# An S4 state-space layer's forward and backward pass: the first quarter of one long transform placed in front of K's return from DRAM, and some transfers issued by another engine

## The chip, the cores and the metric

The kernel runs on one core of a Trainium2 chip. A core has a matrix engine (TensorE, in the profile PE, with its weight loads shown apart as PEld), a vector engine (VectorE, DVE), a scalar engine (ScalarE, ACT), GpSimd (POOL) and SyncE (SP, which here only issues transfers). Transfers between DRAM and the on-chip memory run on 16 DMA engines; SyncE, ScalarE and GpSimd each have a queue in which they issue them, in program order and between their other instructions. Every engine works through its own list of instructions in order and waits on semaphores for the others.

The metric is the time of one execution in microseconds on the device. Three runs of the kernel before took 821.86, 829.3 and 836.6 us; the median is 829.3. The profile comes from one further execution of 824.42 us.

## The reference

One function computes a block and its gradients. `u` is [1, 2048, 512], the state size is N = 128, the feed-forward width F = 1792, and the inputs are bfloat16.

```python
xn = layernorm(A_u)
K  = einsum("dn,dnl,dn->dl", C, exp(dt*A*l), dt*B).real      # a filter of 2048 taps per channel
y  = irfft(rfft(pad(xn)) * rfft(pad(K)))[:L] + xn * Dskip     # long convolution along the sequence
g  = silu( silu(xn @ w1) @ w2 )
out = A_u + y * g
# returned: out, and the gradients of A_u, A_re, A_im, B_re, B_im, C_re, C_im, log_dt, Dskip, w1, w2
```

The backward pass needs two more long convolutions (the gradients to K and to xn), sums over all 2048 positions for the parameters of the state space, and four matrix products for the feed-forward part.

## The kernel before, in words

The kernel computes the Fourier transforms as matrix products with tables of sines and cosines. Positions are split as 128 partitions by T = 16 tiles; frequencies in four quarters `kt` of 512 each; a spectrum quarter is a tile of [128, 2 (real, imaginary), 4, 512] in bfloat16, 1 MB. The order of the work is written out by hand: generators (`gen_xt`, `gen_kt`, `gen_d` and so on) each emit the next piece at a `next`, and the loops of the stages decide whose turn it is. What stands first in that order stands first on every engine's list.

- Stage 1: layer norm, feed-forward forward, the sine tables `TFd` and `TId` in DRAM, and the base powers of the state space, `XYd` in DRAM. It leaves `DS`, the product of the incoming gradient and the gate, on the chip.
- Stage 2 (lines 924 to 1005): for four blocks `b` of channels, `open_tables` (L727) loads base powers into `X`; `chunk_tables` (L769 to 774, and L782 to 789 for the two tables `CY` and `Y`) multiplies them out on VectorE; `chunk_K` (L808) forms the filter K on TensorE; `gen_xt` and `gen_yt` (L878 to 897) transpose the tables and store them as `XTd` and `YTd`. Beside it `fwd_classes` (L919) transforms xn, one quarter at a time; `radix` (L931) finishes a quarter on VectorE with `rad4` (L88) and stores it as `UXd` (L935). `store_K` writes K to DRAM and `load_K` (L833) reads it back in another order as `K_b`, half of the 22 loads on SyncE's queue and half on GpSimd's. Then VectorE adds `Dskip` to one row of `K_b` (L1003). `gen_masks` (L178) is some 60 small VectorE operations.
- Stage 3 (L1143, `gen_kt`): for each quarter, TensorE transforms `K_b` (`fwd_eo`, L1046; ScalarE copies the results out, L1048); VectorE adds even and odd halves (`add_eo`, L1056 to 1061), multiplies by the spectrum of xn (`cplx_mul`, L106 to 110) and runs a radix step (L91 to 98) into `BY`.
- Stage 4 (L1254): eight steps of the inverse transform (`inv_mm`, L1070) give the convolution's result, from which VectorE makes `DO`, the output and more (L1215 to 1217). Woven in is `gen_d` (L1225), the same transform, product and radix step for `DS`, four quarters, into `BK`; the spectra of K and DS are stored as `KXd` and `DXd`.
- Stage 5 (L1441): products for w2's gradient (`Dw2`, L1431) from `DO`; inverse transform of `BK` (L1467), summed over positions by `gs` (L1462) into `dKgd` in DRAM, from where `Gt` is loaded on GpSimd's queue (L1496); `Prod` (L1387) loads `KXd` and `DXd` and forms the third convolution's spectrum `BG` on VectorE. Then the slabs (`Slabs`, L1548) sum for the state-space parameters, with the inverse transform of `BG` and the rest of `Dw2` beside them.
- Stage 6 (L1760): the backward pass of the feed-forward part (`Bwd`), and `gen_ssm_final` (L1303), which loads the sums `Snd` (L1347) and finishes the parameters' gradients on VectorE.

On-chip memory is a stack of pools on a left and a right side (`lo`, `ro`); a tile that is given the place of an older one waits until that one's last reader or transfer is done. A pool with `bufs=1` gives tiles of one `tag` the same place in turn.

Of the kernel before, what the change touches and what calls it, by code (L numbers as in the profile page):

```python
# [11 lines left out]
BF16 = mybir.dt.bfloat16  # L12
# [101 lines left out]
class Stack:  # L114


    def __init__(self, k, side):
        self.k, self.side, self.open_ = k, side, []
# [18 lines left out]
def kernel(ctx, tc, A_u, A_A_re, A_A_im, A_B_re, A_B_im, A_C_re, A_C_im, A_log_dt, A_Dskip, B_x, B_w1, B_w2, grad_out,  # L137
# [26 lines left out]
    k.UXd = XS("UXd"); k.DXd = XS("DXd"); k.KXd = XS("KXd")  # L164
    k.Snd = dr.tile([2, 2, D, N], F32, name="Snd")
# [758 lines left out]
def stage_2(k):  # L924
# [23 lines left out]
    for b in range(NB):  # L948
        Kg = chunk_K(k, b, k.tabs[b])
        Tc, Tn = k.gc.get(b + 1), k.gt.get(b + 1)  # L950
        gx = gen_xt(k, k.xs, b)
        gy = [gen_yt(k, k.xs, i) for i in range(4 * b, 4 * b + 4)]
        sl = [y for g in gy for y in (gx, gx, gx, g)][1:]
        if b == 2:
            sl, gy2 = [None if g in gy else g for g in sl], gy
        if b == 3:
            for _ in Kg:
                pass
            break
        if b:  # L960
            open_tables(k, b + 1, nc.sync)
        fr = front(b + 1) if b else iter(())
        for j, g in enumerate(sl):
            if j % 3 == 1:
                next(fr, None)
            if j < 4:
                next(Tc, None)
            if j == 0 and b < 2:
                next(k.gt[b])
            if j == 4 and b < 2:  # L970
                ld_tab(k, b + 2)
            if j % 2 == 0:
                next(Kg, None)
            if g:
                next(g)
            if b == 0 and j in (1, 3):
                radix(j // 2)
            if j in (4, 6, 8, 10, 12, 14):
                next(Tn)
        for _ in fr:  # L980
            pass
    store_K(k)
    next(k.gt[2])
    for g in gy2:
        next(g)
# [17 lines left out]
    nc.vector.tensor_tensor(out=K_b[0:1, 0, :], in0=K_b[0:1, 0, :], in1=Dsk[:], op=ALU.add)  # L1003
    ro.close("uw", "cyb")
    return K_b, sl
# [101 lines left out]

def gen_kt(k, kq, K_b, UX):

# [5 lines left out]
    def front(kt):  # L1115
        TFs = k.TFs
        TN = neg_tf(k, kq, TFs, False)
        k.TFs = ld_tf(k, (kt + 1) % 4, nc.scalar)
        st[kt] = kq.tile([P, 2, 2, 2, W], BF16, name="Ak", tag="A")
        yield from fwd_eo(k, st[kt], K_b, TFs, TN, False)  # L1120
# [22 lines left out]
def stage_3(k, K_b, sl):  # L1143
# [3 lines left out]
    k.by = lo.open("by")  # L1147
    k.BY = k.by.tile([P, 4, 2, 4, W], BF16, name="BY", tag="B")
    kq = k.kq = lo.open("kq")
    UX = ld_ux(k, kq, 0)  # L1150
    for n, _ in enumerate(gen_kt(k, kq, K_b, UX)):
# [72 lines left out]

def gen_d(k, bk, dp):  # L1225
# [3 lines left out]
    k.BK = []  # L1229
    for kt in range(4):  # L1230
# [15 lines left out]
        B_ = (bk if kt else k.tf2).tile([P, 2, 4, W], BF16, name="BK", tag=f"BK{kt}" if kt else "TFs")  # L1246
# [7 lines left out]
def stage_4(k):  # L1254
# [9 lines left out]
    for t0 in range(0, T, TS):  # L1264
        if t0 % 4 == 0:
            for _ in range(2):
                next(gd)
# [15 lines left out]
        if t0 % 4 == 0:  # L1283
            next(gd)
            if t0 + 4 < T:
                next(gd)
        elif t0 + 2 < T:
            for _ in range(3):
                next(gd)
        else:  # L1290
            next(gd); next(gd)
# [4 lines left out]
        if t0 + 4 == T:  # L1296
            k.w2 = Dw2(k)
            for ft in range(3):
                k.w2.load(ft, nc.gpsimd)
    ro.close("y2")  # L1300


def gen_ssm_final(k, fp):  # L1303
# [83 lines left out]
class Prod:  # L1387


    def __init__(self, k, pw):  # L1390
        self.k, self.ld, self.pl = k, {}, [(k.kq, "A", k.kq, "X"), (k.kq, "UXl", pw, "dXl")]
# [49 lines left out]
def stage_5(k):  # L1441
# [5 lines left out]
    pr = Prod(k, pw)  # L1447
    pr.load(0, k.KXd)
# [16 lines left out]
    for t0 in range(0, T, TS):  # L1465
# [8 lines left out]
        if t0 == 0:  # L1474
            pr.load(1, k.KXd)
        kt = t0 // 4
        if t0 % 4 == 0:
            pr.mul(kt)
        else:
            pr.rad(kt, BG[:, kt])  # L1480
            if kt < 2:
                pr.load(kt + 2, k.KXd)
# [370 lines left out]
```

## Time and profile before

| | us |
|---|---|
| runs shown (3) | 821.86 to 836.6, median 829.3 |
| profiled execution | 824.42 |
| its span, first to last instruction | 822.6 |
| TensorE busy | 676.0 (82%) |
| VectorE busy | 622.5 (76%) |
| ScalarE busy | 435.4 (53%) |
| GpSimd busy | 87.9 (11%) |
| mean granted TensorE clock | 0.929 |

| stretch (us from the start) | what runs |
|---|---|
| 175 to 285 | stage 2: tables, K, transform of xn |
| 285 to 308 | K to DRAM and back |
| 308 to 390 | stage 3: transform of K, `BY` |
| 390 to 480 | stage 4: first inverse transform, `DO`, transform of DS, `BK` |
| 457 to 640 | stage 5 |
| 640 to 822 | stage 6 |

Times below are microseconds from the first instruction of the profiled execution. In a line of the timeline the first number is the start and the second the length; the brackets at its end hold how long the engine had stood idle and what released it. A line may stand for several instructions of one form (x16). "SPq", "ACTq" and "POOLq" are the issues of transfers on the three queues; a transfer's own duration is shown only as "landing", from issue to the end, and only for GpSimd's queue.

### The profile page before, as it was taken

What the parts mean: (1) busy time and instruction counts of PE and PEld (TensorE: products, weight loads), DVE (VectorE), ACT (ScalarE), POOL (GpSimd) and SP (SyncE); (2) the same over time, 40 slices, a digit from 0 to 9 for tenths busy, and PEclk for the clock granted to TensorE, in tenths of its full rate; (3) what the DMA queues carried; (4) which work ended last, traced back from release to release, by engine and by line L of the source; (5) the groups of instructions that cost most, each with busy time, mean ns of one, the idle gap of its engine ahead of it and who ended that gap; (6) DMA issues with size and microseconds to landing.
All of it is one profiled execution on the core that took longest, in us unless ns stands there. A gap on an engine that the chain in (4) does not pass through costs nothing.

```text
span 822.6 us, 13686 instructions
## 1 busy us (share of the span) xinstructions
PE 676.0 (82%) x5284; PEld 345.2 (42%) x5284; DVE 622.5 (76%) x1015; ACT 435.4 (53%) x530; POOL 87.9 (11%) x113
## 2 busy tenths in 40 slices
PE   5868968987478539886999899679887999798998
PEld 2424534434356425342444343234333445344454
DVE  6899999549996992999899999645575458688710
ACT  4888889955569455342444221135444755466221
POOL 1251431020000030000000001102022200001010
PEclk9989979899879878889999999799998999899999
DMA  9557867796788489784788987879999695557561
GB/s 283 203 173 243 293 218 243 269 319 215 255 247 270 116 221 360 288 331 154 239 303 312 366 346 294 186 188 220 269 261 247 157 259 160 156 158 224 179 203 62
DMA packets 154359, 195.19 MB, mean 237 GB/s; under 512 B 37539, under 2 KB 114566, under 8 KB 147862
## 3 DMA queue, kind: packets, MB, share of 16 engines
q1 hardware_dynamic: 144870, 166.26, 65.3%
q0 software_dynamic: 5488, 14.61, 5.8%
q10 hardware_dynamic: 3936, 13.44, 4.8%
q8 instruction: 41, 0.67, 0.3%
q14 instruction: 24, 0.20, 0.1%
HBM read 110.10 MB, written 80.50 MB: 232 GB/s over the span
## 4 chain that ended last, share of the span: by engine, by line
PE 22%; DVE 17%; DMA 12%; ACT 4%; issue 3%; SPq 1%; POOL 0%; DVEq 0%; ACTq 0%; POOLq 0%
PE ps_w L1806 6%; PE ps_v L1070 4%; PE ps_dx L1729 3%; PE ps_da L1690 3%; DMA XTl<-XTd 3%; PE ps_w L1431 2%; DMA Gt<-dKgd 2%; DVE cm_t L106 2%; DMA TIs<-TId 1%; DMA UXl<-UXd 1%; PE ps_V L1584 1%; DMA AW<-akd 1%; PE pt_dh L1712 1%; DMA YTl<-YTd 1%; DVE cm_t L108 1%
## 5 line engine op out<-in xcount | busy, mean ns | idle before, releaser
L579 PE MATMUL ps_h<-XNT,W 128*128 128x512 bf16 x224 | 59.5, 414 | 13.4 <-ACT hs L582 13.4
L1070 PEld LDWEIGHTS <-TIs 128*128 128x128 bf16 x384 | 38.7, 102 | 66.2 <-issue 24.6
L1046 PEld LDWEIGHTS <-TFs 128*128 128x128 bf16 x336 | 34.3, 103 | 62.9 <-issue 28.6
L1431 PE MATMUL ps_w<-DO_all,AW 128*128 128x512 bf16 x224 | 57.1, 405 | 2.9 <-DVE DO_all L1215 2.9
L555 PE MATMUL ps_o<-W,aT 128*128 128x512 bf16 x224 | 54.8, 394 | 2.5 <-DVE ak L76 2.5
L1046 PE MATMUL ps_f<-K_b,TFs 128*128 128x512 bf16 x160 | 43.8, 433 | 14.5 <-DVE K_b L1003 8.1
L1690 PE MATMUL ps_da<-DOT,W2T 128*128 128x512 bf16 x224 | 53.6, 382 | 1.5 <-ACT DOT L1670 1.1
L1729 PE MATMUL ps_dx<-W1T,dhT 128*128 128x512 bf16 x224 | 54.6, 387 | 0.2 <-DMA W1T<-in_B_w_dram 0.2
L1691 DVE TENSOR_TENSOR dhT<-ps_da,sd 128x1024 bf16<-128x1024 f32 x28 | 34.1, 1222 | 23.1 <-ACT sd L133 17.3
L880 ACT COPY XT<-pt_xt 128x1024 bf16<-128x1024 bf16 (+1 forms) x44 | 40.9, 1005 | 17.1 <-DMA XTd<-XT 8.4
L1595 DVE TENSOR_TENSOR T<-Vb,YTl 128x2048 bf16<-128x2048 bf16 x16 | 19.6, 1224 | 39.0 <-ACT Vb L1586 38.9
L1806 PE MATMUL ps_w<-dhc,xn 128*128 128x448 bf16 x256 | 49.1, 352 | 0.0
L1586 ACT CAST Vb<-ps_V 128x1024 bf16<-128x1024 f32 x32 | 31.7, 1013 | 30.8 <-PE ps_V L1584 19.8
L1046 PE MATMUL ps_f<-DS,TFs 128*128 128x512 bf16 x176 | 40.6, 379 | 3.6 <-ACT dEO L1048 2.2
L1070 PE MATMUL ps_v<-BG,TIs 128*128 128x512 bf16 x128 | 33.2, 420 | 8.2 <-DVE BG L97 6.8
L579 PEld LDWEIGHTS <-W 128*128 128x128 bf16 x224 | 22.4, 104 | 38.7 <-issue 21.4
L1738 ACT ACTIVATE dxn<-dxn,c,rstd 128x512 f32<-128x512 f32 x16 | 13.0, 814 | 45.6 <-DVE c L1737 45.6
L1048 ACT CAST Ak<-ps_f 128x1024 bf16<-128x1024 f32 x16 | 16.0, 1014 | 39.1 <-PE ps_f L1046 23.0
L555 PEld LDWEIGHTS <-aT 128*128 128x128 bf16 x224 | 22.8, 102 | 32.1 <-issue 8.3
L1714 ACT COPY dhk<-pt_dh 128x1024 bf16<-128x1024 bf16 x28 | 28.0, 1001 | 14.3 <-PE pt_dh L1712 14.3
L1431 PEld LDWEIGHTS <-AW 128*128 128x128 bf16 x224 | 21.3, 103 | 33.4 <-issue 14.0
L919 PE MATMUL ps_f<-xn,TFs 128*128 128x512 bf16 x128 | 31.8, 401 | 4.2 <-ACT XU L920 2.6
(296 smaller groups left out, 1511.5 us busy)
## 6 DMA issues: line engine op xcount, KB each, us to landing
TIs<-TId SPq DMA_DIRECT2D x24, 512.0 KB
XTd<-XT SPq DMA_DIRECT2D x20, 512.0 KB
XTl<-XTd SPq DMA_DIRECT2D x16, 640.0 KB
UXl<-UXd SPq DMA_DIRECT2D x8, 1024.0 KB
hTd<-hs SPq DMA_DIRECT2D x28, 256.0 KB
akd<-ak SPq DMA_DIRECT2D x28, 256.0 KB
TFs<-TFd ACTq DMA_DIRECT2D x7, 1024.0 KB
hsb<-hTd SPq DMA_DIRECT2D x28, 256.0 KB
```

The lines of the kernel that those rows point to most:

```text
L555: nc.tensor.matmul(out=pso[:], lhsT=aT[:, ft, tt * P:(tt + 1) * P], rhs=W2[:, ft, :], start=(ft == 0), stop=(ft == FT - 1))
L579: nc.tensor.matmul(out=ps[:, j], lhsT=W1[:, dk, ft * P:(ft + 1) * P], rhs=XNT[:, dk], start=(dk == 0), stop=(dk == DK - 1))
L880: nc.scalar.copy(out=XT[:, j0:j0 + len(ks)], in_=pt[:, 0:len(ks)])
L919: nc.tensor.matmul(out=ps[:, c, :], lhsT=TFs[:, t1 + 4 * j, c, :], rhs=src[:, t1 + 4 * j, :], start=(j == 0), stop=(j == 3))
L1046: nc.tensor.matmul(out=ps[:, c, :], lhsT=tab(j), rhs=src[:, t1 + 4 * j, :], start=(n == 0), stop=(n == 4 * len(terms) - 1))
L1070: nc.tensor.matmul(out=ps[:, j, :], lhsT=TIs[:, j, 2 * kt + c, :], rhs=B[kt][:, c, (t0 + j) % 4, :], start=(kt == 0 and c == 0), stop=(kt ...
L1431: nc.tensor.matmul(out=ps[:], lhsT=A[:, t, :], rhs=k.DO[:, t, :], start=(t == 0), stop=(t == T - 1))
L1586: nc.scalar.copy(out=self.V[i][:, g2], in_=ps[:].rearrange("p b c n -> p c b n"))
L1690: nc.tensor.matmul(out=ps[:, j], lhsT=self.W2T[:, dk, ft * P:(ft + 1) * P], rhs=self.DOT[tc_][:, dk], start=(dk == 0), stop=(dk == DK - 1))
L1691: nc.vector.tensor_tensor(out=self.dhT[:, f0:f0 + 2, :], in0=ps[:], in1=sd[:], op=ALU.mult)
L1729: nc.tensor.matmul(out=psx[:], lhsT=dhT[:, ft, t % 4 * P:(t % 4 + 1) * P], rhs=self.W1T[:, ft, :], start=(ft == 0), stop=(ft == FT - 1))
L1806: nc.tensor.matmul(out=ps[:], lhsT=k.xn[:, t, dk * P:(dk + 1) * P], rhs=ch[i][:, t, :], start=(t == 0), stop=(t == T - 1))
```

## The change

Five things are moved; the number of instructions on TensorE and VectorE stays the same.

1. The first quarter of DS (transform, product, radix) leaves stage 4 and stands in stage 2 behind `load_K` and ahead of the `Dskip` addition and the masks (`gen_d0`, new). It uses the table quarter 0 that the first quarter of K also uses, so one load of `TFs` and one of `UXl` go. Its result goes to DRAM (`BKd`, new) and comes back in stage 4. Its two stores are issued by GpSimd.
2. In stage 2, table `Y` of block 2 and its `gen_yt` stand in block 2's own loop; before, they came after K. The radix steps of the third and fourth quarter of xn come right after `store_K`, ahead of table `Y` of block 3; the masks come after the `Dskip` addition.
3. The stores of xn's spectrum (`UXd`) and the loads of `X` for blocks 2 and 3 are issued by GpSimd; before, by SyncE.
4. Stage 4 has three quarters of DS in place of four, the loads for `Dw2` and for the first product of `Prod` stand at step 10, and that product is computed at step 14; in stage 5 the rest of `Prod` moves up accordingly.
5. In `gen_ssm_final` the loads of `Snd` stand four steps earlier.

```diff
     def radix(b):
...
-        nc.sync.dma_start(k.UXd[b], XU[:])
+        nc.gpsimd.dma_start(k.UXd[b], XU[:])
...
         sl = [y for g in gy for y in (gx, gx, gx, g)][1:]
-        if b == 2:
-            sl, gy2 = [None if g in gy else g for g in sl], gy
...
-            open_tables(k, b + 1, nc.sync)
+            open_tables(k, b + 1, nc.gpsimd)
...
-            if j == 0 and b < 2:
+            if j == 0:
                 next(k.gt[b])
...
     store_K(k)
-    next(k.gt[2])
-    for g in gy2:
-        next(g)
+    radix(2); radix(3)
     next(k.gt[3])
-    lo.close("xc", "ko", "sa")
-    k.do = lo.open("do")
+    for _ in range(3):
+        next(gx)
+    ro.close("uw", "cyb"); lo.close("xc", "ko", "sa")
+    k.do = lo.open("do"); k.by = lo.open("by"); kq = k.kq = lo.open("kq")
     K_b = k.do.tile([P, T, D], BF16, name="K_b", tag="DO")
-    Dsk = uw.tile([1, D], BF16, name="Dsk_b", bufs=1)
+    UX = ld_ux(k, kq, 0)
+    Dsk = kq.tile([1, D], BF16, name="Dsk_b")
     nc.sync.dma_start(Dsk[:], k.ins["Dskip"].unsqueeze(0))
     load_K(k, K_b)
-    sl = iter(sl)
-    for n in range(8):
-        next(next(sl))
-        if n == 1:
-            radix(2)
-        if n == 3:
-            radix(3)
-            k.masks = gen_masks(k, uw)
-            next(k.masks)
-    next(k.masks)
+    TN = neg_tf(k, kq, k.TFs, False)
+    d0 = gen_d0(k, kq, UX, TN)
+    for _ in range(4):
+        next(d0)
+        next(gx)
+    next(d0)
     nc.vector.tensor_tensor(out=K_b[0:1, 0, :], in0=K_b[0:1, 0, :], in1=Dsk[:], op=ALU.add)
-    ro.close("uw", "cyb")
-    return K_b, sl
+    for _ in gen_masks(k, kq):
+        pass
+    return K_b, UX, TN, iter([gx] * 4 + gy)
...
+def gen_d0(k, dp, UX, TN):
+    nc = k.nc
+    A = dp.tile([P, 2, 2, 2, W], BF16, name="dEO", tag="A")
+    yield from fwd_eo(k, A, k.DS, k.TFs, TN, False)
+    XD = dp.tile([P, 2, 4, W], BF16, name="XD", tag="X")
+    add_eo(nc, XD, A, half_tmp(k))
+    PX = cplx_mul(nc, k.mm, UX, XD, conj_a=True)
+    nc.gpsimd.dma_start(k.DXd[0], XD[:])
+    B0 = dp.tile([P, 2, 4, W], BF16, name="BK0", tag="X")
+    t = k.mm.tile([P, 2, 4, W], BF16, name="r4_t", tag="cm_t2")
+    E, O = (t[:, i].rearrange("p (c m) w -> p c m w", c=2) for i in range(2))
+    rad4(nc, B0[:, :, 0:2], B0[:, :, 2:4], PX, E, O, True)
+    nc.gpsimd.dma_start(k.BKd, B0[:])
+    yield
...
 def gen_d(k, bk, dp):
     nc = k.nc
-    k.BK = []
-    for kt in range(4):
+    B0 = k.tf2.tile([P, 2, 4, W], BF16, name="BK", tag="TFs")
+    k.BK = [B0]
+    for kt in range(1, 4):
...
+            if n == 0 and kt == 1:
+                nc.sync.dma_start(B0[:], k.BKd)
             yield
...
 def stage_4(k):
...
-        if t0 + 4 == T:
+        if t0 == 10:
             k.w2 = Dw2(k)
             for ft in range(3):
                 k.w2.load(ft, nc.gpsimd)
+            k.pr = Prod(k)
+            k.pr.load(0, k.KXd)
+        if t0 == 14:
+            k.pr.mul(0)
...
 def gen_ssm_final(k, fp):
...
-    yield
-    yield from cmul(CBr, CBi, nat["C_re"], nat["C_im"], nat["B_re"], nat["B_im"])
     S = {}
     for ri in range(2):
         for g2 in range(2):
             S[ri, g2] = q(f"S{ri}{g2}")
             nc.sync.dma_start(S[ri, g2][:], k.Snd[ri, g2].rearrange("(k p) n -> p k n", p=P))
+    yield
+    yield from cmul(CBr, CBi, nat["C_re"], nat["C_im"], nat["B_re"], nat["B_im"])
...
 def stage_5(k):
-    pr = Prod(k, pw)
-    pr.load(0, k.KXd)
+    pr = k.pr
+    pr.pl.append((k.kq, "UXl", pw, "dXl"))
+    pr.load(1, k.KXd)
...
-        if t0 == 0:
-            pr.load(1, k.KXd)
-        kt = t0 // 4
+        kt = (t0 + 2) // 4
         if t0 % 4 == 0:
-            pr.mul(kt)
-        else:
             pr.rad(kt, BG[:, kt])
-            if kt < 2:
-                pr.load(kt + 2, k.KXd)
+        elif kt < 4:
+            pr.mul(kt)
+        if t0 < 4:
+            pr.load(t0 // 2 + 2, k.KXd)
```

More of the change, by code (lines that the diff above doesn't have):

```diff
@@ L973, in stage_2 @@
                 next(Kg, None)
-            if g:
-                next(g)
+            next(g)
             if b == 0 and j in (1, 3):
@@ L1105, in ld_ux, with gen_kt @@
     return UX
-def gen_kt(k, kq, K_b, UX):
+def gen_kt(k, kq, K_b, UX, TN0):
     nc = k.nc
@@ L1140, in gen_kt, with stage_3 @@
         yield
-def stage_3(k, K_b, sl):
+def stage_3(k, K_b, UX, TN, sl):
     nc = k.nc
     lo, ro = k.left, k.right
-    k.by = lo.open("by")
     k.BY = k.by.tile([P, 4, 2, 4, W], BF16, name="BY", tag="B")
-    kq = k.kq = lo.open("kq")
-    UX = ld_ux(k, kq, 0)
-    for n, _ in enumerate(gen_kt(k, kq, K_b, UX)):
+    kq = k.kq
+    for n, _ in enumerate(gen_kt(k, kq, K_b, UX, TN)):
         for g in (next(sl, None) for _ in range(2)):
@@ L1245, in gen_d @@
         yield
[L1246 removed]
+        B_ = bk.tile([P, 2, 4, W], BF16, name="BK", tag=f"BK{kt}")
         t = k.mm.tile([P, 2, 4, W], BF16, name="r4_t", tag="cm_t2")
@@ L1266, in stage_4 @@
             for _ in range(2):
-                next(gd)
+                next(gd, None)
         if t0 >= 4:
@@ L1282, in stage_4 @@
         nc.sync.dma_start(*o)
[L1283 to L1289, printed above, removed]
-        else:
-            next(gd); next(gd)
+        for _ in range(3 if t0 % 4 else 2):
+            next(gd, None)
         if t0 == 4:
@@ L1299, in stage_4 @@
                 k.w2.load(ft, nc.gpsimd)
+            k.pr = Prod(k)
+            k.pr.load(0, k.KXd)
+        if t0 == 14:
+            k.pr.mul(0)
+    assert next(gd, k) is k
     ro.close("y2")
@@ L1387, with __init__ @@
 class Prod:
-    def __init__(self, k, pw):
-        self.k, self.ld, self.pl = k, {}, [(k.kq, "A", k.kq, "X"), (k.kq, "UXl", pw, "dXl")]
+    def __init__(self, k):
+        self.k, self.ld, self.pl = k, {}, [(k.kq, "A", k.kq, "X")]
     def load(self, kt, src):
```

9 lines of the change are left out of this document (4 added, 5 removed).

## The prediction, made before the changed kernel had run

> **What bounds the kernel now.** I read the page's 40 slices first, then the busy time by stretch, then the timeline of the stretches that the change touches, and last what waits for whom. The stretches (columns: TensorE, its weight loads, VectorE, ScalarE, GpSimd, granted clock, DMA share, GB/s) show who is full:
>
> ```profile
> 209.00:230.00 21.00, 5.01 (x66) 4.01 (x63) 20.76 (x47) 9.62 (x12) 0.00 (x0) 0.72 0.91 292
> 308.00:325.00 17.00, 16.98 (x103) 8.58 (x103) 0.25 (x1) 9.04 (x11) 0.00 (x0) 0.83 1.03 361
> 325.00:391.00 66.00, 52.84 (x265) 24.47 (x264) 62.80 (x70) 23.53 (x24) 0.00 (x0) 0.91 0.71 263
> 391.00:460.00 69.00, 67.40 (x308) 29.83 (x307) 64.00 (x85) 29.82 (x32) 1.62 (x3) 0.99 0.82 294
> 480.00:514.00 34.00, 32.97 (x150) 14.13 (x149) 33.69 (x38) 8.15 (x9) 3.50 (x1) 1.00 0.87 328
> ```
>
> VectorE carries the tables and stage 3 (62.80 of 66 us). Stage 4 is full on TensorE and VectorE. Only in 308 to 325 does VectorE stand still. The timeline says why (start, length, engine, line, operation, and in brackets the idle time before it with its releaser):
>
> ```profile
> 261.54 1.09 DVE L769 TENSOR_TENSOR m<-X 128x1792 bf16<-128x1792 bf16 x1 [7.42 <-DMA X<-XYd]
> ...
> 307.56 0.41 DVE L1003 TENSOR_TENSOR K_b<-K_b,Dsk_b 1x512 bf16<-1x512 bf16 x1
> 308.02 6.40 PE L1046 MATMUL ps_f<-K_b,TFs 128*128 128x512 bf16 x16 [8.09 <-DVE K_b L1003]
> ...
> 324.75 0.69 DVE L1056 TENSOR_TENSOR r_t<-Ak 128x1024 bf16<-128x1024 bf16 x1 [16.78 <-ACT Ak L1048]
> ```
>
> So VectorE has two holes: 7.42 us before the tables of the last block, and 16.78 us while TensorE transforms K's first quarter, which itself waited 8.09 us for the one-row addition to K_b. The end of stage 4, the start of stage 5, and a stall in stage 6:
>
> ```profile
> 463.16 9.19 PE L1431 MATMUL ps_w<-DO_all,AW 128*128 128x512 bf16 x34 [2.87 <-DVE DO_all L1215]
> ...
> 475.22 5.77 PE L1070 MATMUL ps_v<-BK,TIs 128*128 128x512 bf16 x26 [1.57 <-DVE BK L97]
> ...
> 497.72 3.63 PE L1070 MATMUL ps_v<-BK,TIs 128*128 128x512 bf16 x16 [0.97 <-DMA TIs<-TId]
> ```
>
> ```profile
> 703.97 0.69 DVE L1332 TENSOR_TENSOR f_big<-nat_B_re,f_big 128x512 f32<-128x512 bf16 x1 [3.54 <-DMA f_big<-Snd]
> ...
> 707.94 1.04 PE L1712 MATMUL pt_dh<-ident_bfloat,dhT 128*128 128x128 bf16 x8 [5.21 <-DVE dhT L1691]
> ```
>
> From 463 to 514.6 TensorE sets the pace; what follows waits for its last ps_g.
>
> **The tables before K.** Y of block 2 (5.3 us, 278.70 to 283.97) moves to 254.1 to 259.4, into the hole of 7.42 us. Y's four copies on ScalarE (1.04 each) follow it ahead of K: ScalarE was through at 274.75 and is now at 278.9, before Kout at 281.31, so they cost nothing with 2.4 us to spare. X of block 3 now comes through GpSimd. SyncE issued it at 256.88, queued behind the YTd store; its last reader on TensorE (L878) ends at 253.0, so GpSimd can issue then. Its issues take 0.57 to 0.92 us each; landings of X on that queue took 5.0 (256 KB) to 11.3 us (512 KB behind 1.7 MB). VectorE needs the first two: 253.0 + 1.5 + 5 gives 259.5, with 10 it is 264.5, against 261.54 now. I take 0 change, the middle; range -2 to +3. VectorE's order behind that point: the column table to 278.7, radix 2 and 3 (5.06 each) to 288.8, Y of block 3 to 294.1. The Trainium skill ("DMA: Bandwidth & Descriptors", Anatomy of one DMA) gives a fit for a GpSimd transfer, 2.0 us plus bytes over 436,000 per us, about 3.2 us here as an estimate; by it this term would be -2, and the trace's 5.0 to 11.3 us say longer.
>
> **The first quarter of DS.** TensorE ends the K chunks at 284.6. Then come six groups of transposes (0.61) and 48 matmuls (16 in 3.62, so 0.226 each): 284.6 + 3.7 + 10.8 = 299.1, and the copy of the fourth PSUM group on ScalarE (1.01) ends at 300. Upper end: its first copy waits for the store of xn's third quarter, which lies where dEO is placed. That store is issued by GpSimd at 284.4; 1 MB landed there in 10.2 us (the row of TFs), so 294.6, then copy, 16 matmuls at the cold 0.4 us of row 308.02, transposes, copy: 303.6. I take 301. VectorE then does add_eo, product and radix: 3.80 + 6.86 + 5.13 = 15.8 us (rows 324.75 to 340.54). The result BK0 takes the buffer of XD, so its two writes wait until GpSimd's store of XD has landed: XD is done at 304.8, issue 0.6, landing 10.2 as above gives 315.6, while VectorE is there at 314.4: 1.2 us (0 at a landing of 5.0, up to 4 behind K_b's loads). Only then, in VectorE's order, stands the addition of Dskip to K_b (0.45): 318.5. All of K's transform is queued behind it on TensorE. K_b itself is in SBUF by 308 now; behind two 1 MB stores it may be some us later and stay hidden. So K starts at 318.5 in place of 308.0: **+10.5** (+8.3 to +14). The masks (7.7 us) move behind the addition, into the hole of 16.8.
>
> The first quarter's TFs load is gone, and one UXl load; a BK store and load come in their place (1 MB each). GpSimd's mask iotas now wait behind the BK store (0.6 us, covered by the hole). SyncE loses the UXd and X issues: its wait for VectorE at 209.75 to 214.47, which starved ScalarE of XT buffers for 8.41 us, goes, but VectorE was 99% busy there, so I price it at 0; without that cover it could give a few us.
>
> **Stage 3** keeps its length: the second quarter's matmuls stand where the first quarter's stood. **Stage 4** loses 15.8 us of VectorE work and 48 matmuls. From the end of BY (389.66) in VectorE's new order: first wait 4.0; eight outputs 8 x 2.06, six products cG 4.1, three quarters 15.4 + 2 x 14.3, Dskip output 1.4, less 1.4 behind the last DO and 1 for short waits: 69.6 us. Now that last DO ends 73.5 us after BY. The gain is only **-3.9**, because the last product and radix (11.7 us) stood behind the last DO and now stand ahead of it. TensorE needs 256 matmuls (58 us) in that time, ScalarE less: neither binds. If the transfers bind (the same MB in less time, 294 GB/s now, 414 the best stretch), the gain is 0.
>
> **Stage 5.** The 34 matmuls of L1431 wait for the last DO. TensorE will have stood still for more than 10 us: 42 matmuls after an idle 6.81 us took 11.93 (row 526.64), so 34 take 10.2, not 9.19: **+1.0** (0 to +2.9). BK is ready: **-1.6**. One pair of 1 MB loads has moved into stage 4: TIs' wait goes, **-1.0** (0 to -1.0). The products on VectorE end earlier, but the load of Gt (landing at 541.4) covers them: 0.
>
> **Stage 6.** The loads of Snd are issued four steps earlier. Matmuls of L1690 start every 3.69 us (693.47, 697.15, 700.84); the next came at 711.75, 7.2 late. VectorE's own work there costs 0.6 elsewhere (716.08). **-6.5** (-4.9 to -7.8).
>
> **Sum**: 0 + 10.5 - 3.9 + 1.0 - 1.6 - 1.0 - 6.5 = -1.5 us. The profiled execution took 824.4 (span 822.6 and 1.8 around it), so 822.9. It lies 4.9 below the median of the three runs, 829.3; from there **827.8**.
>
> A rule speaks against the stores on GpSimd. First the row:
>
> ```profile
> L833 POOL DMA_DIRECT2D K_b<-Kud x11: 504/559/1336, 292.9 to 299.1; - x11
> ```
>
> The median issue took 559 ns while VectorE was busy 6.38 of 7.10 us. The Trainium skill ("SBUF — State Buffer", the "DVE blocks DMA" trap) says that VectorE in its two-port modes keeps GpSimd from writing descriptors, with 620 ns becoming 3100, but excepts tensor_tensor; if it held for these too, eleven issues would be some 27 us longer, an estimate; the row says not.
>
> **Rivals.**
> 1. *VectorE's lead counts.* Its holes shrink from 7.4 + 16.8 to 2.0 + 6.9 (294.1 to 301) + 1.2 + 9.0 (masks end 326.2, KX at 335.2, 16.7 behind K's start) = 19.1, so its work is done 5.1 us earlier. If that and not TensorE set stage 5: -5.1 - 6.5, **817.7**. For: stage 3 is VectorE's. Against: ps_v and ps_g run nearly without a gap from 475 to 514.6.
> 2. *Slower: K_b comes late.* GpSimd's half of K_b's loads stands behind the stores of xn's last two quarters on one queue. If each takes 10.2 us in turn (284.4, 294.6, 304.8) and the half then needs its 14 us (292.9 to about 307), K_b is whole at 319 to 324. It decides from 318.5 on, and the kernel is slower than before from 320. At 324: +16 - 3.9 + 1.0 - 2.6 - 6.5 = +4, **833.3**. For: the 10.2 us row, DMA share 1.08 in 300 to 308. Against: DMA share 0.02 in 278.8 to 285.4, so the stores start on free engines.
> 3. *Stage 4 gives nothing* (transfers): +3.9 on the sum, **831.7**. Against: 0.82 DMA share.
> 4. *The moved stores matter* by the starved ScalarE at 215 to 223: a few us, inside the range, as VectorE has no gap there.
>
> **Chances**: forecast 0.55, VectorE's lead 0.15, K_b late 0.20, stage 4 nothing 0.10. Terms all at their kind ends give -8 (821), less the 7.4 by which a single run left the median (821.86 to 836.6): 814. Above, rival 2 plus 5 for the runs: 839. A measurement of this kernel tells about 2% from no change; that is 812.7 and 845.9. No case lies outside by itself; with the runs' spread rival 1 gives most of 0.12 faster, rival 2 of 0.08 slower, and 0.80 stays within 2%.
>
> **What the new profile would show.** The K_b addition at 315 to 320, right behind the radix of the first quarter, TensorE idle for over 10 us before K's first matmul; VectorE idle about 9 us before KX instead of 16.8; no wait for Snd; the L1431 matmuls waiting for DO by more than 2.87 us. I am wrong if K starts before 313 (then the gain is real), if a K_b load ends that wait, or if stage 4 is not VectorE's.

## The result, and the profile after

The changed kernel takes 835.5 us (median of 16 runs, 830.4 to 839.0), the kernel before beside it 828.9 (16 runs, 821.9 to 836.6). The ratio is **1.0082, with a 95% interval of 1.0059 to 1.0104**: 6.6 us slower, inside what was called no change (2%), but clearly on the other side of the forecast of -1.5 us. A later series gave 1.0086 (1.0053 to 1.0119). The ratios leave out runs more than 1.5% above the fastest of the same kernel; of the kernels tried, this touches only the one with three edits together, where it leaves out two of ten, the profiled one among them.

The profiled execution took 838.2 us (span 836.4), 2.8 above its median, that of before 4.5 under its own; so the two profiles differ by 13.8 us where the medians differ by 6.6. A second profile of the changed kernel, taken in that series, has a span of 831.0. Both are used.

The timeline of the changed kernel, first profile, at the places that the prediction showed for before (start, length, engine, line, operation; in brackets the idle time ahead of it and what ended it):

```profile
301.42 0.69 DVE L1052 TENSOR_TENSOR r_t<-dEO 128x1024 bf16<-128x1024 bf16 x1 [8.49 <-ACT dEO L1044]
...
307.27 2.70 POOL L834 DMA_DIRECT2D K_b<-Kud  x3 [6.38 <-DMA K_b<-Kud]
309.94 0.58 POOL L1228 DMA_DIRECT2D DXd<-XD  x1
...
322.28 1.23 DVE L97 TENSOR_TENSOR BK<-r_t 128x2048 bf16<-128x2048 bf16 x1 [7.63 <-DMA DXd<-XD]
...
324.56 0.40 DVE L998 TENSOR_TENSOR K_b<-K_b,Dsk_b 1x512 bf16<-1x512 bf16 x1
325.02 6.51 PE L1042 MATMUL ps_f<-K_b,TFs 128*128 128x512 bf16 x16 [24.23 <-DVE K_b L998]
...
341.99 0.69 DVE L1052 TENSOR_TENSOR r_t<-Ak 128x1024 bf16<-128x1024 bf16 x1 [8.57 <-ACT Ak L1044]
...
437.54 7.43 PE L1042 MATMUL ps_f<-DS,TFs 128*128 128x512 bf16 x20 [3.54 <-DMA TFs<-TFd]
...
482.50 10.15 PE L1444 MATMUL ps_w<-DO_all,AW 128*128 128x512 bf16 x34 [1.84 <-DVE DO_all L1209]
...
500.37 0.58 ACT L1448 CAST AW<-ps_w 128x512 bf16<-128x512 f32 x1 [10.55 <-DMA out_dram<-AW]
...
501.94 1.45 PE L1476 MATMUL ps_g<-dK,gs_s 128*128 128x512 bf16 x6 [2.38 <-ACT dK L1482]
```

The addition to K_b does stand behind the first quarter's work, as forecast, and TensorE waits 24.23 us for it. But inside that work VectorE waits 7.63 us for the store of XD, which GpSimd issued only at 309.94, behind three loads of K_b that had themselves waited 6.38 us. The second profile has the same picture with smaller waits:

```profile
318.26 1.23 DVE L97 TENSOR_TENSOR BK<-r_t 128x2048 bf16<-128x2048 bf16 x1 [2.52 <-DMA DXd<-XD]
320.54 0.41 DVE L998 TENSOR_TENSOR K_b<-K_b,Dsk_b 1x512 bf16<-1x512 bf16 x1
...
321.00 6.02 PE L1042 MATMUL ps_f<-K_b,TFs 128*128 128x512 bf16 x16 [21.30 <-DVE K_b L998]
...
432.33 5.84 PE L1042 MATMUL ps_f<-DS,TFs 128*128 128x512 bf16 x20 [2.97 <-DMA TFs<-TFd]
```

From such rows the difference can be laid out by stretches (in us against the profile of before; the two right columns add up to the differences of the spans, 836.4 - 822.6 and 831.0 - 822.6):

| stretch | forecast | first profile | second profile |
|---|---|---|---|
| to K's first matmul | +10.5 | +17.0 | +13.0 |
| to the end of BY (stage 3) | 0 | +0.3 | -0.1 |
| to the end of the last DO (stage 4) | -3.9 | +2.1 | -0.3 |
| to the last ps_g (start of stage 5) | -1.6 | +1.5 | +2.5 |
| to stage 6 | 0 | +0.1 | +0.5 |
| stage 6 | -6.5 | -7.2 | -7.2 |
| sum | -1.5 | +13.8 | +8.4 |

By these profiles three rows are off: K's start by 2.5 to 6.5, stage 4 by 3.6 to 6.0, the start of stage 5 by 3 to 4 us. But the profile of before is one execution, and a quick one. The kernel before with part 5 alone, run twice below, has the order of before up to stage 6. In its two profiles K started at 309.64 and 309.33; from the end of BY to the last DO it took 73.9 and 74.0 us (73.5 in the profile of before), and from there to the last ps_g 54.2 and 53.9, where the profile of before took 50.7 and the changed kernel 52.3 and 53.2. The second of them:

```profile
309.33 6.05 PE L1046 MATMUL ps_f<-K_b,TFs 128*128 128x512 bf16 x16 [8.03 <-DMA K_b<-Kud]
...
484.91 2.72 PE L1462 MATMUL ps_g<-dK,gs_s 128*128 128x512 bf16 x6 [2.34 <-ACT dK L1468]
```

So the start of stage 5 is no later than the unchanged order takes by itself. Two rows remain: K's start, over the forecast by 1 to 6.5 us according to the profile it is compared with, and stage 4, by 3 to 6.

Busy time by stretch of the first profile (columns as in the prediction):

```profile
308.00:325.00 17.00, 0.00 (x0) 0.00 (x0) 9.29 (x12) 0.00 (x0) 2.59 (x5) 0.50 0.87 216
325.00:342.00 17.00, 16.98 (x109) 8.92 (x110) 7.02 (x58) 8.81 (x10) 0.84 (x4) 0.83 0.43 146
342.00:407.00 65.00, 52.14 (x265) 24.20 (x264) 63.02 (x70) 24.82 (x25) 0.00 (x0) 0.91 0.72 268
408.00:477.00 69.00, 59.75 (x259) 25.89 (x257) 58.29 (x76) 25.25 (x27) 1.59 (x3) 0.92 0.80 278
```

In 308 to 325 TensorE does nothing while the DMA engines are 87% busy. Then, in K's first quarter, VectorE has only the masks (7.02 of 17 us) and DMA falls to 0.43. Stage 4 (the last row; 391 to 460 in before) is no longer full on any engine: TensorE 59.75 and VectorE 58.29 of 69 us, against 67.40 and 64.00.

### The profile page after: what moved, and what is told of

Its sections match the earlier page's. It is cut to its first block, busy times and chain, and to the rows that moved or that the text cites. A ratio compares the mean times of both kernels' runs of the same rounds, so it can differ in the third digit from the quotient of the medians.

```text
span 836.4 us, 13705 instructions
## 1 busy us (share of the span) xinstructions
PE 676.3 (81%) x5284; PEld 344.3 (41%) x5284; DVE 623.0 (74%) x1015; ACT 434.3 (52%) x529; POOL 96.6 (12%) x129
## 4 chain that ended last, share of the span: by engine, by line
PE 25%; DMA 13%; DVE 12%; ACT 3%; issue 3%; SPq 1%; POOL 0%; ACTq 0%; DVEq 0%; POOLq 0%
PE ps_w L1818 6%; PE ps_f L1042 4%; DMA XTl<-XTd 4%; PE ps_v L1066 4%; PE ps_dx L1741 3%; PE ps_da L1702 3%; PE ps_w L1444 2%; DMA AW<-akd 2%; DMA Gt<-dKgd 2%; DVE cm_t L106 1%; DMA TFs<-TFd 1%; DMA TIs<-TId 1%; DMA dhd<-dhk 1%; PE ps_V L1596 1%; DVE dhT L1703 1%
## 5 line engine op out<-in xcount | busy, mean ns | idle before, releaser
L1444 PE MATMUL ps_w<-DO_all,AW 128*128 128x512 bf16 x224 | 59.8, 418 | 10.2 <-DVE DO_all L1209 10.2
L1741 PE MATMUL ps_dx<-W1T,dhT 128*128 128x512 bf16 x224 | 52.9, 379 | 0.0
L1042 PE MATMUL ps_f<-DS,TFs 128*128 128x512 bf16 x176 | 43.5, 399 | 5.6 <-DMA TFs<-TFd 3.5
L1596 PE MATMUL ps_V<-XTl,Gbd 82*32 82x256 bf16 x512 | 20.4, 292 | 22.4 <-DVE Gbd L1584 12.7
L1584 DVE TENSOR_TENSOR Gbd<-Gt,MK 82x512 bf16<-82x512 bf16 x32 | 20.5, 681 | 23.6 <-DMA Gt<-dKgd 23.6
L809 PE MATMUL ps_k<-X,CY 128*32 128x41 bf16 x1024 | 21.6, 248 | 19.7 <-DVE CY L788 15.3
```

The lines of the kernel that those rows point to most:

```text
L1042: nc.tensor.matmul(out=ps[:, c, :], lhsT=tab(j), rhs=src[:, t1 + 4 * j, :], start=(n == 0), stop=(n == 4 * len(terms) - 1))
L1444: nc.tensor.matmul(out=ps[:], lhsT=A[:, t, :], rhs=k.DO[:, t, :], start=(t == 0), stop=(t == T - 1))
L1741: nc.tensor.matmul(out=psx[:], lhsT=dhT[:, ft, t % 4 * P:(t % 4 + 1) * P], rhs=self.W1T[:, ft, :], start=(ft == 0), stop=(ft == FT - 1))
```

## The experiments

All ratios are to the kernel before, run beside them on the same chip (its median there 825.8 for the first four runs, 826.9 for the next four, 827.6 for the rest). Two theories stood at the start. **A**: K waits for the first quarter's VectorE work and the buffer that BK0 shares with XD, while K_b itself lies ready. **B**: K_b itself comes late (the prediction's second rival).

### BK0 in its own buffer

```diff
-    B0 = dp.tile([P, 2, 4, W], BF16, name="BK0", tag="X")
+    B0 = k.by.tile([P, 4, 2, 4, W], BF16, name="BK0", tag="B")[:, 0]
```

> The changed kernel with one edit: the first quarter's result BK0 lies in BY's place, so its write no longer waits for the store of XD. Theory A (the shared buffer and the addition's place are what delays K, K_b itself lies ready by about 315): the 7.6 us wait of VectorE goes, the addition runs at about 317 in place of 324.6, K starts 7 us earlier, and the time falls from 835.5 to about 828.5 (ratio to the kernel before 0.999). Theory B (K_b itself comes late: the last GpSimd load was issued at 309.3 and such loads landed after 10.4 us): the addition now waits for a K_b load until about 320, K starts 4 us earlier, 831.5 (ratio 1.003).

Measured: 832.0, ratio 1.0083 (1.0050 to 1.0116). The addition ran at 317.0, but only two matmuls followed; the other fourteen of the first group waited for a load of K_b until 319.50. By the time, no gain can be told.

### The addition to K_b ahead of the first quarter's VectorE work

```diff
-    next(d0)
     nc.vector.tensor_tensor(out=K_b[0:1, 0, :], in0=K_b[0:1, 0, :], in1=Dsk[:], op=ALU.add)
+    next(d0)
```

> The changed kernel with one edit: the addition of Dskip to K_b stands ahead of all of the first quarter's VectorE work, so K starts as soon as K_b has landed, and the first quarter's product and radix run beside K's first 17 us of matmuls. Theory A: K_b lies ready when VectorE comes (301 to 315), K starts at about 313 to 315, 10 to 12 us earlier than at 325.0: 824 to 826 (ratio 0.995). Theory B: VectorE waits for a K_b load until about 320, K starts 4 us earlier: 831.5 (ratio 1.003), and the product and radix, 15.8 us and a wait for XD's store, then end at about 340, near K's first quarter at 338, so up to 3 us of it can be lost again.

Measured: 832.4, ratio 1.0060 (1.0031 to 1.0090). The timeline of this run:

```profile
305.50 0.41 DVE L997 TENSOR_TENSOR K_b<-K_b,Dsk_b 1x512 bf16<-1x512 bf16 x1 [10.70 <-DMA K_b<-Kud]
...
315.89 1.01 PE L1042 MATMUL ps_f<-K_b,TFs 128*128 128x512 bf16 x2 [16.14 <-DMA K_b<-Kud]
319.98 5.89 PE L1042 MATMUL ps_f<-K_b,TFs 128*128 128x512 bf16 x14 [3.07 <-DMA K_b<-Kud]
```

With nothing of the first quarter in the way, the last load of K_b still ends TensorE's wait only at 319.98, against 308 at the latest in before. **Theory A falls: K_b is some 12 us late by itself**, and the VectorE work and the wait for XD's store lie beside that. By the time, this run can't be told from the changed kernel.

### Stores of xn's spectrum and loads of X back on SyncE

```diff
-        nc.gpsimd.dma_start(k.UXd[b], XU[:])
+        nc.sync.dma_start(k.UXd[b], XU[:])
...
-            open_tables(k, b + 1, nc.gpsimd)
+            open_tables(k, b + 1, nc.sync)
```

> The changed kernel with part 3 undone: the stores of xn's spectrum and the loads of X for blocks 2 and 3 are issued by SyncE again; the rest as changed. Theory A: they cost nothing, same time within 2 us (835.5, ratio 1.008). Theory B with GpSimd's queue as the reason (two 1 MB stores ahead of half of K_b's loads on one queue): K_b is whole earlier, the wait for XD's store becomes shorter as well, and K starts 3 to 7 us earlier (829 to 833); with the amount of transfers as the reason: no change in K's start, and X of block 3 comes later by up to 2 us (835.5 to 838).

Measured: 835.2, ratio 1.0109 (1.0078 to 1.0140); K started at 321.26, as in the second profile of the changed kernel. So part 3 is worth nothing either way that these runs can tell. About K_b itself the run says less: GpSimd issued its last three loads at 301.32 in place of 307.27, but VectorE waited 2.74 us for XD's store, and that hides when K_b was whole. Whether the two stores on GpSimd's queue, on which the prediction's second rival put the blame, delay K_b is answered by the run with UXl moved, below: with both stores still on that queue its last three loads went out at 300.33 after a wait of 0.28 us.

### The table load, and xn's load, out of K_b's way

K_b's landing times point at a suspect. The view of one tile's instructions gives, for GpSimd's half of its 22 loads, the least, median and greatest time from issue to landing; before:

```profile
DMA to landing us min/median/max: 2.8/3.7/8.0
```

and changed:

```profile
DMA to landing us min/median/max: 9.8/10.4/11.0
```

Two loads of 1 MB now run beside them: UXl, on SyncE's queue ahead of K_b's own loads, and the next table quarter TFs, on ScalarE's. In before and in the changed kernel:

```profile
308.60 0.36 ACTq L611 DMA_DIRECT2D TFs<-TFd  x1
315.51 3.17 SPq L1104 DMA_DIRECT2D UXl<-UXd  x1
```

```profile
291.84 1.70 SPq L1100 DMA_DIRECT2D UXl<-UXd  x1
300.89 0.36 ACTq L612 DMA_DIRECT2D TFs<-TFd  x1
```

There is a second step: late landings delay later issues. In before GpSimd issued its eleven loads in one go, by 299.70:

```profile
292.87 6.85 POOL L833 DMA_DIRECT2D K_b<-Kud  x11 [109.42 <-DMA YTd<-YT]
```

In the changed kernel it issued eight, and the last three only at 307.27, when an earlier one had landed. SyncE's half was held as well, by UXl on its own queue; the view of what the issues waited for (total, times, longest):

```profile
SPq L834 <- DMA UXl<-UXd: 5.9, 1, 5.9
```

In the second profile this wait is 7.2 us.

First, TFs alone: ScalarE issues the load after K's first group of matmuls.

```diff
-        k.TFs = ld_tf(k, kt % 3 + 1, nc.scalar)
+        if kt:
+            k.TFs = ld_tf(k, kt % 3 + 1, nc.scalar)
...
-        yield from fwd_eo(k, st[kt], K_b, TFs, TN, False)
+        for n, _ in enumerate(fwd_eo(k, st[kt], K_b, TFs, TN, False)):
+            if n == 0 and kt == 0:
+                k.TFs = ld_tf(k, 1, nc.scalar)
+            yield
```

> The changed kernel with the load of the next table quarter alone moved (TFs, 1 MB, issued by ScalarE after K's first group of matmuls, not at 300 us); buffer of BK0 and place of the addition as changed. If the amount of transfers beside K_b's loads is the cause: XD's store and the last K_b loads land earlier, K starts at 317 to 319 in place of 321, and the time falls by 2 to 4 us against the changed kernel (ratio 1.004 to 1.006). If the gain of the run with three edits came from the other two: 1.008.

Measured: 832.5, ratio 1.0055 (1.0027 to 1.0084), by its middle 2 us less than the changed kernel's, though the intervals overlap. GpSimd's loads of K_b landed after 8.3 us in the median. That alone doesn't blame TFs: with TFs early they took 8.1 in the run with BK0's own buffer and 9.0 in the kernel without part 5. K started at 321.67, since VectorE still waited 4.34 us for XD's store. Which is why the same edit was also run together with the two edits above:

> The changed kernel with BK0 in its own buffer, the addition to K_b ahead of the first quarter's VectorE work, and the load of the next table quarter (TFs, 1 MB, issued by ScalarE at 300.9, in the middle of K_b's loads) issued only after K's first group of matmuls. Theory B with the amount of transfers as the reason: 1 MB of about 6 that moved from 296 to 325 goes out of K_b's way; at the 230 GB/s of that stretch that is 4.3 us, so K's matmuls run from 316 in place of 320: ratio 1.002 to 1.004. If K_b is late by the two stores on GpSimd's queue or by its own scattered packets: 320 as before, ratio 1.006.

Measured: 827.4, ratio 0.9972 (0.9932 to 1.0011); K's matmuls ran from 318.15, 2.9 us earlier than in the second profile of the changed kernel, and BY was finished 4.5 us earlier. The size is uncertain: its ten runs lie between 817.2 and 832.6, and the profiled one, of 832.6, has a span of 830.8, no shorter than the second profile of the changed kernel (831.0). Still it is the first of these runs that can't be told slower than before, and the three edits together give some 7 us by the medians. K_b was whole at 318.15, against 319.50 and 319.98 in the two runs above that show it with TFs early: TFs is worth 1 to 2 us of the 12.

Then UXl behind K_b's loads as well:

```diff
-    UX = ld_ux(k, kq, 0)
     Dsk = kq.tile([1, D], BF16, name="Dsk_b")
     nc.sync.dma_start(Dsk[:], k.ins["Dskip"].unsqueeze(0))
     load_K(k, K_b)
+    UX = ld_ux(k, kq, 0)
```

> As the run with TFs later, and the load of xn's first quarter (UXl, 1 MB) is issued behind K_b's loads on SyncE's queue in place of ahead of them; so no load of 1 MB stands in K_b's way any more. Theory B, amount of transfers: K's matmuls run from 309 to 313 (before: 308.0), some 8 to 10 us earlier than in the runs with TFs and UXl early, and the time is 823 to 826 against 826 to 829 of the kernel before (ratio 0.995 to 0.999). If the reason is another, K stays at 316 to 320 and the ratio at 1.003 to 1.006.

Measured: 835.3, ratio 1.0089 (1.0059 to 1.0119).

```profile
310.34 1.01 PE L1042 MATMUL ps_f<-K_b,TFs 128*128 128x512 bf16 x2 [9.71 <-DMA K_b<-Kud]
315.39 5.55 PE L1042 MATMUL ps_f<-K_b,TFs 128*128 128x512 bf16 x14 [4.04 <-DMA K_b<-Kud]
...
318.13 2.29 DVE L106 TENSOR_TENSOR cm_t<-XD,UXl 128x4096 bf16<-128x4096 bf16 x1 [13.10 <-DMA UXl<-UXd]
```

GpSimd's loads of K_b landed after 5.0 us in the median, and K ran from 315.39, between the two figures of the expectation. So moving both loads takes back 4 to 5 of the 12 us; the other 7 are left. Some of these can lie with UXl, which now runs beside K_b's last loads, and with K's own return, which begins later (its first load was issued at 295.70, in before at 292.87); no run separates them. And now UXl, issued at 302.85, landed at 318.13; VectorE waited 13.10 us for it, and the first of KX came at 340.1, later than with UXl early (334.3). The load had only changed places with those it had held up.

### The same load put on the kernel before

```diff
+    nc.sync.dma_start(k.Scr[0], k.UXd[0])
+    nc.scalar.dma_start(k.Scr[1], k.UXd[1])
     load_K(k, K_b)
```

> The kernel before with two copies of 1 MB from DRAM to DRAM (of xn's first two quarters to a place nobody reads) issued by SyncE and ScalarE just ahead of K_b's loads; nothing else. It puts beside K's return what the changed kernel puts there (UXl and TFs, 1 MB each). If the amount of transfers is the cause: K_b's loads land after 8 to 11 us in place of 3.7, the last of them are issued later because only eight of a queue are under way at a time, K starts at 314 to 320 in place of 308, and the time rises by 5 to 10 us (ratio 1.006 to 1.012). If the transfers do not hinder each other: 308 to 310 and ratio 1.000 to 1.002.

Measured: 834.8, ratio 1.0073 (1.0052 to 1.0094), that is 6.0 us more.

```profile
295.32 5.49 POOL L834 DMA_DIRECT2D K_b<-Kud  x9 [111.12 <-DMA YTd<-YT]
303.02 1.34 POOL L834 DMA_DIRECT2D K_b<-Kud  x2 [2.21 <-DMA K_b<-Kud]
...
313.48 1.03 PE L1049 MATMUL ps_f<-K_b,TFs 128*128 128x512 bf16 x2 [6.04 <-DMA K_b<-Kud]
318.31 5.49 PE L1049 MATMUL ps_f<-K_b,TFs 128*128 128x512 bf16 x14 [3.80 <-DMA K_b<-Kud]
```

**Two transfers of 1 MB beside K's return, and nothing else, make K 8 us late** (318.31 against 308.02, less 2.1 by which this execution was behind already at the end of table CY) and the kernel slower by nearly as much as the change does. Even the wait of the last loads for an earlier one appears (2.21 us). This settles theory B, and shows that two such transfers are enough. It does not show that their amount alone does it: the copies run from DRAM to DRAM, where UXl and TFs load the on-chip memory, and one stands ahead of K_b's loads on SyncE's queue, as UXl does. SyncE's half began only at 301.91 (295.29 in before), since the issue of the Dskip load ahead of it took 4.01 us (0.34 in before), and it then waited 1.9 us for the copy; GpSimd's half landed after 6.2 us, not 10.4. What the engines shared and what the order of a queue held up was not separated.

### The last table of stage 4 ahead of time

The chain of work that ended last, in the first profile of the changed kernel, goes through stage 4 so (start, length, what):

```profile
413.29 13.83 PE ps_f L1042 x64
427.20 10.30 DMA TFs<-TFd
437.54 16.93 PE ps_f L1042 x64
454.47 3.47 PE ps_v L1066 x16
457.96 1.03 ACT S_s L1289
```

The table of the last quarter of DS has the place of the one in use, since BK0 occupies the other table buffer; it can be asked for only at 427.20 and takes 10.30 us. In before the load in the same place was issued at 428.13 and in use at 434.78 without a wait:

```profile
428.13 0.33 ACTq L611 DMA_DIRECT2D TFs<-TFd  x1
...
434.78 3.62 PE L1046 MATMUL ps_f<-DS,TFs 128*128 128x512 bf16 x16
```

So the load is asked for no later than before and lands later. From 427 to 438 the DMA engines were 0.74 busy in before and 0.97 in the changed kernel, where a load of UXl was issued just ahead, at 426.55 (431.81 in before). The edit lets BK0 come back later and loads that table into the other buffer while the second is in use:

```diff
-    B0 = k.tf2.tile([P, 2, 4, W], BF16, name="BK", tag="TFs")
-    k.BK = [B0]
+    k.BK = [None]
...
-            if n == 3 and kt < 3:
-                k.ntf += 1
+            if n == (3 if kt == 1 else 0) and kt < 3:
                 k.TFs = ld_tf(k, kt + 1, nc.scalar)
-            if n == 0 and kt == 1:
-                nc.sync.dma_start(B0[:], k.BKd)
+            if n == 0 and kt == 3:
+                k.BK[0] = k.tf2.tile([P, 2, 4, W], BF16, name="BK", tag="TFs")
+                nc.sync.dma_start(k.BK[0][:], k.BKd)
```

> The changed kernel with one edit in stage 4: the last table quarter of DS is loaded while the second is in use (BK0 comes back into the other table buffer later), so that the wait of 3.54 us for TFs at 437.5 goes. From the end of BY to the last DO the changed kernel took 75.5 us where 69.6 was forecast and 73.5 was measured before. If that wait and what follows from it on VectorE (3.98 and 1.82 us) make the difference: 70 to 72 us, and 3.5 to 5 us off the total. If VectorE's own work at the end of the stage binds anyway, or the other transfers: 74 to 75.5 and nothing off.

Measured: 831.0, ratio 1.0042 (1.0013 to 1.0071), 3.9 us under the changed kernel beside it (834.9); the two intervals overlap a little. From the end of BY to the last DO it took 70.2 us: the 69.6 that the prediction had reckoned. The wait moves on but costs less:

```profile
459.55 5.31 PE L1066 MATMUL ps_v<-BY,TIs 128*128 128x512 bf16 x15 [5.19 <-DMA TIs<-TId]
```

### All four edits; and K_b's largest loads first

> Four edits of the changed kernel together: BK0's own buffer, the addition to K_b early, TFs later, and the table of the last quarter of DS loaded ahead in stage 4. If the gains of the single runs add up (1.0086 as changed; 1.000 by the medians of the run with the first three; 3.6 us for the fourth): 822 to 824 against 827, ratio 0.994 to 0.997. If stage 4 then waits for something else: 1.000.

Measured: 824.3, ratio 0.9952 (0.9934 to 0.9970): faster than before, and by the ratios 11 us under the changed kernel. The gains add up within the intervals.

```diff
         dma(K_b[0:16, 8 * k1:8 * k1 + 8], g0[k1])
+    for o, (r0, r1) in enumerate(((0, 5), (5, 12), (12, 16))):
+        dma(K_b[64:128, r0:r1], U[512 + o:512 + o + 127:2].unsqueeze(1).to_broadcast([64, r1 - r0, D]))
...
-    for o, (r0, r1) in enumerate(((0, 5), (5, 12), (12, 16))):
-        dma(K_b[64:128, r0:r1], U[512 + o:512 + o + 127:2].unsqueeze(1).to_broadcast([64, r1 - r0, D]))
```

> As the run with four edits, and K_b's three largest loads (64 rows each, 256 to 448 KB) are issued third to fifth in place of last, so that they are not the ones that wait for a free place of eight. If the late issue of the large ones is what makes K_b late: K's matmuls run 2 to 5 us earlier than with four edits, ratio 0.990 to 0.995. If the engines are simply full: the same as with four edits.

Measured: 824.7, ratio 0.9967 (0.9947 to 0.9987). K's first matmuls ran earlier (310.2 to 316.0 in place of 314.7 to 318.2) and the time did not fall. The reason is on VectorE, which in both runs comes from the first quarter and the masks to K's transform without a wait; here in the second:

```profile
308.62 0.41 DVE L997 TENSOR_TENSOR K_b<-K_b,Dsk_b 1x512 bf16<-1x512 bf16 x1 [13.66 <-DMA K_b<-Kud]
...
333.31 0.68 DVE L1052 TENSOR_TENSOR r_t<-Ak 128x1024 bf16<-128x1024 bf16 x1
```

With the four edits alone that instruction starts at 333.51, hardly later. ScalarE's last copy of K's first quarter had ended at 328.6 (333.0 with the four edits). So K's matmuls no longer set the pace here: VectorE does, which stands 13 us in front of the addition to K_b and works through the moved quarter only after it.

### Part 5 alone, parts 1 to 4 alone

> The kernel before with part 5 alone: the four loads of Snd are issued four steps earlier. If the step of stage 6 as reckoned is right, the stall of TensorE near 701 to 708 goes and the time falls by 6.5 to 7.1 us, to 822 (ratio 0.992). If something else is late in its place, less: 0 to 3 us.

Measured: 820.3, ratio 0.9926 (0.9881 to 0.9971). Again, in the last series:

> The kernel before with part 5 alone, again, beside the next two on one chip. As in its first run: ratio 0.991 to 0.994 (820 to 822 where the kernel before takes 827).

Measured: 820.4, ratio 0.9927 (0.9905 to 0.9949), **7.2 us less than before**. And without part 5:

> The changed kernel without part 5 (the loads of Snd stand where they stood): parts 1 to 4 alone. If part 5 is worth the same in both kernels, 0.7 to 0.8%: ratio 1.015 to 1.017, so parts 1 to 4 cost 12 to 14 us, twice what the whole change costs. If part 5 is worth less behind parts 1 to 4: 1.009 to 1.012.

Measured: 842.3, ratio **1.0202** (1.0163 to 1.0241): parts 1 to 4 cost 14.7 us by the medians (six runs; 13 to 20 by the interval), more than expected, and part 5 hides about half of it. The stall that part 5 removes is back in this run:

```profile
725.99 1.03 PE L1724 MATMUL pt_dh<-ident_bfloat,dhT 128*128 128x128 bf16 x8 [5.88 <-DVE dhT L1703]
```

Last, the four edits beside part 5 alone on one chip:

> The changed kernel with the four edits, again, beside the kernel before with part 5 alone. If the move of the first quarter gains something once its transfers and the table wait are out of the way: under the time of the kernel before with part 5 alone, by 1 to 4 us. If K's start, still some 8 us later than before, eats what stage 4 gives: 2 to 4 us over it (ratio 0.995).

Measured: 825.2, ratio 0.9977 (0.9956 to 0.9998), 4.8 us over part 5 alone. So even with these edits parts 1 to 4 cost more than they give. The wait for K's return is not gone in it: in its profile VectorE stood 12.36 us and TensorE 14.99 us for loads of K_b. Whether the moved quarter gains where that wait is short was not tried. **The fastest kernel of the study is the one before with the four loads of Snd moved, and nothing else.**

The changed kernel itself was run a second time for its second profile (told above):

> The changed kernel as it is, once more, for a second profile and a time beside the next runs. In its first profile K started at 325.0 with a wait of 7.6 us for XD's store; in the two runs that took that wait away K's matmuls really ran from about 320, and the time hardly fell. If the wait is always there, K starts at 325 again and this run is 3 to 4 us slower than a run with the wait away; if it is an accident of that one execution, K starts at 319 to 322. Time 832 to 835 (ratio 1.008).

The wait for XD's store is always there, but its size varies (7.63, 2.52, and 4.71 us in the kernel without part 5), and it decides K's start only where it ends after K_b is whole, at about 320: by some 5 us in the first profile, by 1 or 2 in the other two.

## Why the prediction was wrong, point by point

The forecast was -1.5 us (827.8); it is +6.6. The range (814 to 839; its upper sum, 833.3 plus 5, is really 838.3) held the time, and no difference beyond 2% was right. Two terms failed, both by taking for granted that a transfer lands as it did before: K's start, +10.5 (the wait for BK0 and the time at which K_b is whole), and stage 4, -3.9 ("1 for short waits"). The second alone, 3 to 6 us, turns the sign.

- **Tables before K**: priced at 0; table CY of the last block ended 1.3 us earlier in one profile and 0.3 later in the other. Right.
- **K's start, +10.5**: measured +17.0 and +13.0 against the profile of before, 11.4 to 15.7 against the two profiles with part 5 alone. The step that failed is the sentence "K_b itself is in SBUF by 308 now; behind two 1 MB stores it may be some us later and stay hidden". Where the runs show it, it was in SBUF at about 320. It did stay hidden behind the first quarter's work, but that this is as long is luck: without that work K's matmuls run no earlier than 320. The prediction looked for what delays K_b among the stores on GpSimd's queue; K's start didn't change without them. It had counted which loads appear and disappear over the whole kernel (one TFs and one UXl fewer), not that a UXl and a TFs are now issued 24 and 8 us earlier, into K's return. How much of the 12 us is the engines' sharing and how much the order on SyncE's queue stays open.
- **BK0's wait, 1.2 (0 to 4)**: 7.6, 4.7 and 2.5. The landing was priced well (10.2 forecast, 12.2 and 8.7 measured); the issue was not: 309.9 and 309.5 in place of 304.8, because the prediction let GpSimd issue when XD was ready and left out that K_b's loads on its queue would be waiting. In the second profile 2.22 us more went to a wait for UXl, which the prediction does not have.
- **Stage 4, -3.9**: +2.1 and -0.3. The count of VectorE's work was right (69.6 forecast, 70.2 with the table ahead of time, against 75.5 and 73.2). What failed is "1 for short waits": one table load, which had just fitted before, now ended 3.54 and 2.97 us late, and VectorE waited behind it for ScalarE. "If the transfers bind ... the gain is 0" was named, and given 0.10.
- **Start of stage 5, +1.0 - 1.6 - 1.0**: the matmuls of Dw2 took 10.15 us in the first profile, as forecast (10.2), but 33 of them 9.35 in the second. The wait for BK went, and ps_g waited 2.38 and 2.55 us for ScalarE, which stood 10.55 us for a store of AW ahead of its copies of dK. But the order of before has that wait too in another execution (2.34 us, shown above), and there it needs as long in all. The wait for TIs was there again (0.97 and 1.04). The small terms here can't be told from the spread between executions, and the forecast's -1.6 took one profile for the rule.
- **Stage 6, -6.5**: -7.2 in both profiles, -7.3 and -7.5 with part 5 alone. Right.
- **Rivals**: the second (K_b at 319 to 324, 833.3) described the outcome best, with a reason that the runs don't bear out; the third (stage 4 gives nothing) came true beside it. They had been weighed as alternatives, 0.20 and 0.10. Both happened where the DMA engines were fuller than before (0.71 busy while GpSimd issued its loads of K_b in before, 1.05 from 296 to 308 in the changed kernel; 0.74 and 0.97 at the table load), and they came together: +3.9 on 833.3 would have been 837. The first (VectorE's lead) did not show, and the fourth did not show in the run with SyncE. GpSimd's issues of K_b took 567 ns in the median, against 559 before; by that, the rule of the Trainium skill ("SBUF — State Buffer", the "DVE blocks DMA" trap) was rightly held not to bear on this VectorE work.

## What to carry to other kernels

Work moved into a wait brings its loads with it. If the wait is for transfers, those loads lengthen it, and the hole that looked free on the compute engines is the place where the DMA engines are full: look at the DMA row of the stretch before its VectorE row, and list the transfers by when they are issued, not by whether they exist. Two rivals that rest on the same resource belong in one case, with their prices added. And a change of several parts should be run in parts: here four of five cost 14.7 us, and the fifth, four lines moved, was the whole gain.

## What the runs showed of the hardware that was not expected

Beside the two added loads, the size of a transfer said little about its landing. A load of K_b of 1 KB on GpSimd's queue, in the view of transfers (name, queue, count, size, us to landing), in before:

```profile
K_b<-Kud POOLq DMA_DIRECT2D x1, 1.0 KB, 3.6
```

and in the first profile of the changed kernel, where a load of 320 KB took 10.0 (7.6 in before):

```profile
K_b<-Kud POOLq DMA_DIRECT2D x1, 1.0 KB, 10.6
```

The Trainium skill ("DMA: Bandwidth & Descriptors", Anatomy of one DMA) gives 2.0 us plus bytes over 436,000 per us for such a transfer: an estimate of 2.0 us for 1 KB and 4.4 for 1 MB. The trace comes near it for the two stores of xn's spectrum (1 MB, 4.8 us in the median, the DMA engines 0.79 busy from 283 to 293). It is far from it for XD's store (1 MB, 12.2 us, the engines 1.02 busy), and above it for the 1 KB load in both kernels.

A full DMA share is also no measure of bytes: from 296 to 325 us the engines were busy 1.02 of the time in before and moved 311 GB/s, and 0.95 and 0.94 in the two profiles of the changed kernel, at 217 and 258 GB/s. Why so much fewer bytes pass was not tried.
